# Two of eight expert weight loads split into a 112-partition transfer and five small ones

## The chip, the cores and the metric
One NeuronCore of a Trainium2 chip runs the whole kernel. The metric is device time in microseconds (us), the median of several executions; lower is better. The core has five instruction engines (PE for matmuls, DVE, ACT, POOL, SP) and 16 DMA engines that carry every transfer between HBM and the core's memory (SBUF). A transfer that POOL issues goes into the software queue q0; one that SP or ACT issues goes into a hardware queue, q1 or q10.

## What is computed
Sliding-window attention (plain in heads 0 to 3, dilated by 4 in heads 4 to 7) over 8 batches of 576 tokens, and behind it a soft mixture of experts with 32 slots, four for each of 8 experts:

```python
x = attn_out.transpose(0, 2, 1, 3).reshape(4608, 512)
logits = x @ phi                      # 4608 x 32
d = softmax(logits, axis=0); c = softmax(logits, axis=1)
slot_input = (d.T @ x).reshape(8, 4, 512)
for e in range(8):
    slot_out[e] = relu(slot_input[e] @ w1[e]) @ w2[e]   # w1: 512 x 1024, w2: 1024 x 512
return c @ slot_out.reshape(32, 512)
```

All inputs and the output are float32 in HBM. w1 and w2 of one expert are 2 MB each there, and 1 MB each as float16 in SBUF.

## The kernel before
**Stages.** The attention runs as 32 units, four for each batch (two heads at a time), each with transposes, scores, a softmax and values; the logits, token weights and slot sums of a batch follow some units behind. Then come the eight experts in pairs: `expert_in` (w1), `expert_turn` (transposes of the hidden values), `expert_out` (w2, summed into `sop`). Last, the 13 output tiles: a matmul of the token weights with `so`, a scaling by ACT or DVE into `ot`, and a store that SP issues (L791). The weights are so late, and the output so large, that the last expert's w2 and the slot output are done in two sides of 256 columns: side 0 of `so` is ready, and five output tiles' left halves are sent, before side 1 of w2 of expert 7 has arrived.

**Loads.** Apart from the first two and a table of constants, all loads are issued by POOL in an order written out by hand, because they cast float32 to float16 on the way. First the eight batches of q, k and v (`load_batch`), into eight large tiles `home0` to `home7`. When the attention has used up a home, w1 and w2 of an expert go into its two halves: in unit 4e+2, `load_w1(e)` for e up to 6 and `load_w2(e)` for e up to 4; after the loop w1 of expert 7 and w2 of experts 5, 6 and 7. For experts 0 to 5 `load_w2` is one transfer of 128 partitions; each partition is one row of 8 x 512 values, 16 KB in HBM and 8 KB in SBUF. The w2 of experts 6 and 7 are cut by columns, into three and four transfers.

**Order and limits.** POOL works in program order. The framework gives POOL's transfers eight completion semaphores in turn, so that a transfer can be issued when the one eight before it has landed. Between the weight loads POOL only clears four small tiles `hTp` (L643) for the turned hidden values. An instruction that reads a weight tile waits for the transfers that wrote it.

**Engines.** The transfers run on the 16 DMA engines at once; a transfer of 128 partitions gives each of them eight rows. Each DMA engine takes its own share from the queue in order and goes on to the next transfer without waiting for the others. A transfer has landed when all 16 have marked it complete.

Of the kernel before, what the change touches and what calls it, by code (L numbers as in the profile page):

```python
# [37 lines left out]
OUT_COLS = [sum(nj for _, nj in OUT_TILES[:i]) for i in range(len(OUT_TILES))]  # L38
NU = 4 * B
NV = 2  # L40
SIDES = ((0, DMODEL // 2), (DMODEL // 2, DMODEL))
PIECES = ((0, 6), (6, 8))
HALF = 4
# [16 lines left out]
def kernel(  # L60
# [10 lines left out]
    nc = tc.nc  # L71
# [15 lines left out]
    for n, (nm, ten, by) in enumerate((("qp", q, nc.sync), ("kp", k, nc.scalar))):  # L87
        first[nm] = stage[0:NP, 768 * n : 768 * n + 768].rearrange("p (g x) -> p g x", g=2)
        by.dma_start(
            out=first[nm],  # L90
            in_=ten[0, 0:2].rearrange("h s d -> (h s) d").rearrange("(g p r) d -> p g (r d)", g=2, r=RP),
# [3 lines left out]
    def kept(shape, name, dt=FP16):  # L95
        return keep.tile(shape, dt, name=name, tag=name)
# [24 lines left out]
    ends = kept([128, 2, 130], "ends")  # L121
    vp = [kept([128, NKB + 1, 4, D + 1], f"vp{i}") for i in range(NV)]
    vd = [kept([128, 16, D + 1], f"vd{i}") for i in range(2)]
# [9 lines left out]
    for i in range(2):  # L133
        nc.vector.memset(vd[i][:, :, D : D + 1], 1.0)
    for i in range(NV):
        nc.vector.memset(vp[i][:, :, :, D : D + 1], 1.0)
# [72 lines left out]
    def select_v(b):  # L209
        raw, last = raws[b]["vp"], raws[b]["vt"]  # L210
        for i in range(2):
            sel = ps_s.tile([128, 2, 2, 4, D], FP32, name=f"sel{b}_{i}", tag="s")
            for r in range(4):
                for n in range(2):
# [8 lines left out]
                    )  # L223
            nc.scalar.copy(out=vp[b % NV][:, 2 * i : 2 * i + 2, :, 0:D], in_=sel[:, :, 0])
        end = ring.tile([128, 2, 4, D], FP32, name=f"sel{b}_2", tag="ring")
        for r in range(4):
# [7 lines left out]
            )  # L234
        nc.scalar.copy(out=vp[b % NV][:, 4:6, :, 0:D], in_=end)

# [9 lines left out]
    def load_half(e, side):  # L246
        d0, d1 = SIDES[side]
        nc.gpsimd.dma_start(
            out=w_tiles[e][1][:, HALF:8, d0:d1],
            in_=moe_w2[e].rearrange("(p c) f -> p c f", p=128)[:, HALF:8, d0:d1],  # L250
        )

    def load_w2(e):
        w2t = w_tiles[e][1]
        w2_from = moe_w2[e].rearrange("(p c) f -> p c f", p=128)
        if e == E_EXP - 2:
            nc.gpsimd.dma_start(
                out=w2t[:, 0:HALF].rearrange("p c f -> p (c f)"),
                in_=w2_from[:, 0:HALF].rearrange("p c f -> p (c f)"),
            )  # L260
            load_half(e, 0)
            return
        if e < E_EXP - 2:
            nc.gpsimd.dma_start(
                out=w2t.rearrange("p c f -> p (c f)"), in_=w2_from.rearrange("p c f -> p (c f)")
            )
            return
        w2t = w_tiles[e][1] = w2t.rearrange("p c f -> p (c f)").rearrange("p (s c f) -> p s c f", s=2, c=8)
        for n, (d0, d1) in enumerate(SIDES):
            if n == 1:  # L270
                load_half(e - 1, 1)
            for c0, c1 in PIECES:
                nc.gpsimd.dma_start(out=w2t[:, n, c0:c1], in_=w2_from[:, c0:c1, d0:d1])
# [148 lines left out]
    def values(u):  # L422
# [11 lines left out]
        for h in range(2):  # L434
            mms = []
            for blk in range(NKB):
                if plain:
                    mms.append((blk, Pp[:, h, blk, 0:128], vp[b % NV][:, blk, hl + h, :]))
                    if blk > 0:
                        mms.append((blk, Pp[:, h, blk - 1, 128:256], vp[b % NV][:, blk - 1, hl + h, :]))  # L440
                elif blk < 4:
# [100 lines left out]
    def front_slots(b, up=None):  # L542
# [3 lines left out]
        for n in range(9):  # L546
            j = n % 4
            d0, d1 = (0, DMODEL) if n == 8 else SIDES[n // 4]
            nc.tensor.matmul(  # L549
# [15 lines left out]
    def last_slots(last, dcs):  # L565
        er, x = Er[(B - 1) % 2], xs[B - 1]
        for dc in dcs:
            to = last[:, N_SLOTS * dc : N_SLOTS * dc + N_SLOTS]
            for blk in range(4):
                for g in range(2):  # L570
                    d0, d1 = SIDES[g]
                    nc.tensor.matmul(
# [42 lines left out]
    for u in range(NU - 2):  # L615
        st = scores(u + 1)
        if u + 3 < NU:
            regroup(u + 3)
        values(u)
        softmax_parts(u + 1, st)  # L620
        if u + 3 < NU:
            transposes(u + 3)
        b, ph = divmod(u - 4, 4)
        if b >= 0:
            if ph == 1:
                front_logits(b)
            elif ph == 2:
                front_rows(b)
            elif ph == 3:
                front_slots(b)  # L630
        if u == 1:
            spread_phi()
        if u >= 1:
            x_transposes(u - 1)
        if u % 4 == 3 and u // 4 + 1 < B:
            spread_v(u // 4 + 1)
            select_v(u // 4 + 1)
        if u % 4 == 2 and u // 4 < E_EXP - 1:
            load_w1(u // 4)
            if u // 4 < E_EXP - 3:  # L640
                load_w2(u // 4)
        if 26 <= u:
            nc.gpsimd.memset(hTp[u - 26], 0.0)  # L643

    load_w1(E_EXP - 1)
    load_w2(E_EXP - 3)
    load_w2(E_EXP - 2)
    load_w2(E_EXP - 1)

# [25 lines left out]
    for c in range(2):  # L675
# [14 lines left out]
        out=siT,  # L690
# [45 lines left out]
    def expert_out(e, side=None, chs=range(8)):  # L736
        d0, d1 = (0, DMODEL) if side is None else SIDES[side]
        w2t = w_tiles[e][1][:, side] if e == E_EXP - 1 else w_tiles[e][1][:, :, d0:d1]
        for ch in chs:
            j = ch % 4  # L740
            nc.tensor.matmul(
                sop[32 * j : 32 * j + 32, d0:d1],
                hTp[e % 4][:, ch, 28 - 4 * e : 60 - 4 * e],
                w2t[:, ch, :],
                start=(e == 0 and ch < 4),
                stop=(e == E_EXP - 1 and ch >= 4),
                skip_group_check=True,
            )
# [43 lines left out]

    for n, (d0, d1) in enumerate(SIDES):
        expert_out(E_EXP - 2, n, range(HALF, 8))
# [40 lines left out]
```

## Time and profile before

| What | Value |
|---|---|
| Time, median of 3 runs | 181.5 us (181.28 to 181.54) |
| The profiled execution: its time | 181.12 us |
| The profiled execution: its span | 179.4 us |
| Busy: PE, DVE, ACT, POOL | 145.9, 124.1, 116.2, 52.9 us |
| PE clock granted, mean | 0.902 |
| q0 (POOL's transfers) | 24416 packets, 30.68 MB |
| q1 (outputs, and one first load) | 4592 packets, 9.82 MB |
| w2 as one transfer: POOL's time to issue it (L264) | 0.53 to 0.54 us |

The span is what the instruction engines' records cover; the execution's own time is 1.7 us longer. A packet record in the trace has a start, a duration, a size and a queue, but no DMA engine's number. The completion marks of each transfer are in the trace too, 16 for each transfer.

### The profile page before, as it was taken

How to read it: one execution, taken by the hardware profiler on the slowest of the kernel's cores; microseconds unless marked ns; L12 is line 12 of the kernel's file. 1: busy time of each engine (PE TensorE's matmuls, PEld its weight loads, DVE VectorE, ACT ScalarE, POOL GpSimd, SP SyncE). 2: the span in 40 equal slices, each digit the busy share in tenths (PEclk: the TensorE clock that was granted, in tenths of full speed). 3: DMA queues.
4: the chain of work that ended last, by engine and by line, in shares of the span. 5: the costliest groups of instructions: out<-in, count | busy, mean ns of one | idle time of the engine just before them, and what ended most of it. 6: DMA issues, size and time to landing. Idle time of an engine off the chain costs nothing.

```text
span 179.4 us, 5142 instructions
## 1 busy us (share of the span) xinstructions
PE 145.9 (81%) x2138; PEld 98.0 (55%) x2138; DVE 124.1 (69%) x341; ACT 116.2 (65%) x216; POOL 52.9 (30%) x86
## 2 busy tenths in 40 slices
PE   6549988999989989989998998998888997797000
PEld 2324666777576667667666757765658343342000
DVE  7407699689799978978979979876862011799200
ACT  2236768687888789789789788877721131699100
POOL 7946545454554644401110005006111100000000
PEclk9975699579999999999999999999998599999755
DMA  5999999999999999999999999999999999999995
GB/s 154 193 199 202 202 203 201 201 203 202 203 202 201 202 201 204 219 221 210 212 225 212 216 219 212 217 216 210 223 214 214 212 194 192 264 384 422 433 425 227
DMA packets 29238, 41.11 MB, mean 229 GB/s; under 512 B 1696, under 2 KB 26400, under 8 KB 26784
## 3 DMA queue, kind: packets, MB, share of 16 engines
q0 software_dynamic: 24416, 30.68, 98.0%
q1 hardware_dynamic: 4592, 9.82, 14.1%
q10 hardware_dynamic: 208, 0.29, 0.6%
q8 instruction: 16, 0.26, 0.5%
q14 instruction: 6, 0.05, 0.1%
HBM read 62.02 MB, written 9.44 MB: 398 GB/s over the span
## 4 chain that ended last, share of the span: by engine, by line
PE 30%; DMA 28%; DVE 17%; ACT 9%; issue 5%; POOL 3%; DVEq 0%; ACTq 0%; POOLq 0%
DMA home<-in_moe_w_dram 24%; PE o L448 6%; DMA home<-in_v_dram 4%; PE rgx L468 4%; ACT qT L305 4%; DVE ot L788 4%; PE sel L227 3%; PE l L486 3%; ACT pr L369 3%; PE s L343 3%; DVE x L453 3%; DVE P L395 2%; PE f L782 2%; DVE kTd L320 2%; PE u L549 2%
## 5 line engine op out<-in xcount | busy, mean ns | idle before, releaser
L453 DVE TENSOR_TENSOR x<-o,rc 128x640 f16<-128x640 f32 x32 | 26.3, 821 | 0.4
L369 ACT ACTIVATE pr<-s 128x960 f16<-128x960 f32 (+1 forms) x32 | 22.9, 761 | 1.6 <-PE s L343 1.6
L376 ACT ACTIVATE pd<-s 128x640 f16<-128x640 f32 x32 | 22.0, 713 | 2.1 <-PE s L352 2.0
L171 POOL DMA_DIRECT2D home<-in_v_dram x24 | 16.6, 692 | 14.9 <-DMA home<-in_k_dram 8.8
L448 PE MATMUL o<-vd,P 128*128 128x65 f16 x256 | 14.5, 198 | 3.2 <-DVE x L453 2.6
L240 POOL DMA_DIRECT2D home<-in_moe_w_dram x8 | 4.2, 531 | 40.8 <-PE rgq L315 33.4
L474 ACT COPY xT<-rgx 128x512 f16<-128x512 f16 x16 | 9.4, 586 | 10.2 <-PE rgx L468 10.2
L448 PEld LDWEIGHTS <-P 128*128 128x128 f16 x288 | 12.2, 100 | 6.8 <-DVE x L453 3.6
L385 DVE TENSOR_TENSOR Pp<-pr,fixed 128x1280 f16<-128x1280 f16 (+1 forms) x32 | 15.4, 497 | 0.3 <-ACT pr L369 0.3
L448 PE MATMUL o<-vp,Pp 128*128 128x65 f16 x288 | 15.3, 201 | 0.0
L468 PE MATMUL rgx<-fixed,x 128*128 128x128 f16 x155 | 14.0, 222 | 1.3 <-DVE x L453 0.6
L448 PEld LDWEIGHTS <-Pp 128*128 128x128 f16 x288 | 12.0, 102 | 4.1 <-issue 2.4
L788 DVE TENSOR_SCALAR ot<-f,rrow 128x256 f32<-128x256 f32 (+1 forms) x24 | 12.8, 610 | 2.1 <-PE f L782 2.1
L305 ACT COPY qT<-rgq 128x576 f16<-128x576 f16 x16 | 10.2, 639 | 6.1 <-PE rgq L304 5.4
L395 DVE TENSOR_TENSOR P<-pd,fixed 128x1024 f16<-128x1024 f16 x16 | 10.8, 672 | 4.7 <-ACT pd L376 4.7
L468 PEld LDWEIGHTS <-x 128*128 128x128 f16 x160 | 10.1, 98 | 6.6 <-issue 4.2
L786 ACT ACTIVATE ot<-f,rrow 128x256 f32<-128x256 f32 (+1 forms) x24 | 11.9, 601 | 2.5 <-PE f L782 1.7
L320 ACT COPY qT<-rgq 128x576 f16<-128x576 f16 x16 | 10.2, 640 | 4.1 <-PE rgq L315 4.0
L782 PE MATMUL f<-so,ET 128*128 128x256 f16 (+1 forms) x48 | 10.7, 324 | 2.3 <-ACT ot L786 1.1
L320 DVE COPY kTd<-rgk 128x576 f16<-128x576 f16 x16 | 12.3, 772 | 0.0
L197 POOL DMA_DIRECT2D home<-in_k_dram x15 | 10.0, 667 | 7.8 <-DMA home<-in_q_dram 7.1
L315 PEld LDWEIGHTS <-home 96*128 96x128 f16 x192 | 10.4, 103 | 3.3 <-DMA home<-in_q_dram 2.0
(119 smaller groups left out, 319.4 us busy)
## 6 DMA issues: line engine op xcount, KB each, us to landing
home<-in_moe_w_dram POOLq DMA_DIRECT2D x14, 1024.0 KB, 28.0
out_dram<-ot SPq DMA_DIRECT2D x5, 1024.0 KB, 7.8
home<-in_q_dram POOLq DMA_DIRECT2D x15, 288.0 KB, 9.8
home<-in_k_dram POOLq DMA_DIRECT2D x15, 288.0 KB, 9.9
home<-in_v_dram POOLq DMA_DIRECT2D x16, 256.0 KB, 9.8
out_dram<-ot SPq DMA_DIRECT2D x8, 256.0 KB, 2.9
out_dram<-ot SPq DMA_DIRECT2D x4, 512.0 KB, 7.2
home<-in_moe_w_dram POOLq DMA_DIRECT2D x2, 384.0 KB, 22.5
```

The lines of the kernel that those rows point to most:

```text
L171: nc.gpsimd.dma_start(out=dst, in_=v[b, h0 : h0 + n_h, r0 : r0 + 4 * n_p, :].rearrange("h (p r) d -> p h (r d)", r=4),)
L305: nc.scalar.copy(out=dst[:, 0:S].rearrange("c (p r) -> c p r", r=RP), in_=rg.rearrange("c r p -> c p r"),)
L320: (nc.scalar.copy if nm == "q" else nc.vector.tensor_copy)(out=dst[:, 0:S].rearrange("c (g p a) -> c g p a", g=4, a=3), in_=rg.rearrange(" ...
L369: nc.scalar.activation(out=(pr[:, :, 0 : 3 * QW], pr[:, :, 3 * QW :])[part], in_=st[:, :, 0 : (480, 224)[part]], func=AF.Exp, scale=SCALE,)
L376: nc.scalar.activation(out=pr[:, part].rearrange("p c e t -> p e c t"), in_=st[:, :, 0 : 2 * DW].rearrange("p e (c t) -> p e c t", c=2), f ...
L385: nc.vector.tensor_tensor(out=Pp[:, :, b0 : b0 + nb, 0:w], in0=pr[:, :, b0 * QW : b0 * QW + nb * w].rearrange("p h (t c) -> p h t c", c=w) ...
L395: nc.vector.tensor_tensor(out=P1.rearrange("p a c t -> p (a c) t"), in0=pr[:, :, :, 0:128].rearrange("p a c t -> p (a c) t"), in1=mask[:, ...
L448: nc.tensor.matmul(ot[:, h, blk], lhs, rhs, start=(n == 0), stop=(n == len(mms) - 1), skip_group_check=True)
L453: nc.vector.tensor_tensor(out=xs[b][:, :, 2 * D * hp : 2 * D * hp + 2 * D].rearrange("p t (h d) -> p h t d", h=2), in0=ot[:, :, :, 0:D], i ...
L468: nc.tensor.transpose(rg[:, 128 * blk : 128 * blk + 128], x[:, blk, hl : hl + 128], ident)
L782: nc.tensor.matmul(fp, ET[:, c0 : c0 + 127 * nj + 1 : nj], so[:, d0:d1], start=True, stop=True)
L788: nc.vector.tensor_scalar(out=ot[:, j], in0=fp, scalar1=scale, scalar2=None, op0=ALU.mult)
```

## The change
For experts 1 and 4 the one transfer of w2 becomes six, issued in this order. Together they name each of the 128 x 4096 values once.

```diff
+UNEVEN = (
+    (0, 112, 0, 4096), (126, 128, 0, 256), (112, 120, 0, 4096),
+    (120, 128, 256, 512), (120, 128, 512, 4096), (120, 126, 0, 256),
+)
...
         if e < E_EXP - 2:
-            nc.gpsimd.dma_start(
-                out=w2t.rearrange("p c f -> p (c f)"), in_=w2_from.rearrange("p c f -> p (c f)")
-            )
+            whole = w2t.rearrange("p c f -> p (c f)"), w2_from.rearrange("p c f -> p (c f)")
+            pieces = UNEVEN if e in (1, 4) else ((0, 128, 0, 4096),)
+            for p0, p1, x0, x1 in pieces:
+                to, of = (ap[p0:p1, x0:x1] for ap in whole)
+                nc.gpsimd.dma_start(out=to, in_=of)
             return
```

The entries of `UNEVEN` are first and last partition and first and last column. The transfer of 112 partitions is seven rows for each of 16 engines. The other five carry partitions 112 to 127. Two of them are large (eight whole rows, and eight rows of 3584 columns) and three are small (2, 8 and 6 rows of 256 columns, 512 bytes each in SBUF). If a transfer of n partitions, n below 16, takes n engines, the next ones in turn, then the leading transfer of two moves the turn on by two; the two large ones, with eight between them, fall on the same eight engines, two further than with eights alone; and after 2 + 8 + 8 + 8 + 6 = 32 the turn is where it was.

## Prediction
> **What bounds the kernel now.** I read the page's slices and queues first, then the stretch between the last load and the first output in short windows, then the timeline there, then POOL's issues.
>
> ```profile
> span 179.4 us, 5142 instructions
> ...
> DMA  5999999999999999999999999999999999999995
> ...
> q0 software_dynamic: 24416, 30.68, 98.0%
> q8 instruction: 16, 0.26, 0.5%
> q14 instruction: 6, 0.05, 0.1%
> ```
>
> The DMA engines are busy in all slices but the first and the last, so the kernel ends when the last of them has carried its share. The two lines "instruction" are program text, fetched by the same engines.
>
> ```profile
> core 0: us, PE busy (x) PEld busy (x) DVE busy (x) ACT busy (x) POOL busy (x), PEclk, DMA share, GB/s
> 151.50:152.00 0.50, 0.11 (x6) 0.10 (x1) 0.00 (x0) 0.34 (x1) 0.00 (x0) 1.00 1.44 194
> 152.00:152.50 0.50, 0.41 (x4) 0.38 (x4) 0.00 (x0) 0.14 (x2) 0.00 (x0) 1.00 1.15 155
> 153.00:153.50 0.50, 0.50 (x4) 0.31 (x4) 0.50 (x2) 0.50 (x3) 0.00 (x0) 1.00 0.83 113
> 153.50:154.00 0.50, 0.50 (x4) 0.16 (x2) 0.50 (x2) 0.50 (x3) 0.00 (x0) 1.00 0.75 99
> 154.50:155.00 0.50, 0.40 (x6) 0.11 (x6) 0.45 (x2) 0.19 (x1) 0.00 (x0) 1.00 1.10 366
> ```
>
> DMA share is the last figure but one; it passes 1 because packets overlap. From 152.0 it sinks to half of its 1.44: the engines do not finish their loads together. The last load's 16 completion marks say by how much. In us after the first they are 0, 0.05, 0.06, 0.32, 0.59, 0.86, 1.14, 1.65, 2.07, 2.28, 2.39, 2.45, 2.50, 2.59, 2.65 and 2.88.
>
> Why: q8 has 16 packets of 16 KB, 893 to 974 ns each, the last at 148.6. After each fetch the marks of the following transfers show one engine some 1.1 us later than before, and the second eight fetches hit the same eight engines as the first (their durations also repeat in eights). So eight engines are hit twice, 2.2 us each: the last eight marks. The eight others have the first eight marks. The one at 1.65 among these was already 1.22 us behind the first engine at 14 us into the span, and an 8 KB fetch of q14 (322 ns) delayed it once more.
>
> ```profile
> start us, us, engine line op out<-in xcount [idle before <-releaser]
> 150.89 0.73 PE L741 MATMUL sop<-home,hTp 128*32 128x512 f16 x16 [0.27 <-DVE hTp L731]
> 151.66 0.37 ACT L796 CAST so<-sop 128x256 f16<-128x256 f32 x1 [3.65 <-PE sop L741]
> 153.08 2.63 SPq L791 DMA_DIRECT2D out_dram<-ot  x4
> 155.24 0.29 PE L741 MATMUL sop<-home,hTp 128*32 128x256 f16 x2 [0.28 <-DMA home<-in_moe_w_dram]
> ```
>
> The first output is not held by a load: side 0 of w2 of expert 7 landed at 151.24, and PE's work of side 0, which came from the turned values (L731), ran until 151.6. SP's first store follows at 153.08 and its first packets at 154.35. Twelve engines were then idle and began at once; four still had loads and began at 154.53, 154.59, 154.67 and 154.91. From there all of them send without a pause. The first output's marks are 0.61 us apart and the last one's 0.57, with the second latest 0.26 and 0.24 before the latest. **So the latest engine alone sets the end**, with 0.56 us (154.91 less 154.35) before PE's chain would set it instead.
>
> **The change, part by part.** (1) Rows moved. A 1 MB weight transfer takes 4.87 us from landing to landing; less its closing word of 0.022 us and over eight rows this is 0.606 us for a row. The eight engines of the large pieces get 7 + 1 + 3584/4096 = 8.875 rows, the others 7 + 2 x 256/4096 = 7.125, where all had 8. For two experts that is 2 x 0.875 x 0.606 = 1.06 us more on eight engines, and 1.06 less on eight.
>
> (2) Closing words. q0 has 1248 packets of 4 bytes for 78 transfers, 16 each, 22 ns until the next packet; also for the eight v loads of 16 partitions, the narrowest. Ten more transfers cost each engine 10 x 0.022 = 0.22 us if every engine posts one, and nothing at the lower end, if only engines with data do (two words an expert in place of one come to 0.02). I take 0.22, by the nearest row.
>
> The Trainium skill (DMA: Bandwidth & Descriptors, "Why a DMA increments its semaphore by 16 and not by 1") says that on POOL's path all 16 engines post, whatever the shape. By it this term is 0.22; no trace here has a narrower transfer to show it.
>
> (3) POOL issues ten more transfers, 10 x 0.54 = 5.4 us at the price of L264, and the window of eight transfers holds fewer bytes:
>
> ```profile
> 85.70 0.53 POOL L264 DMA_DIRECT2D home<-in_moe_w_dram  x1 [4.31 <-PE rgk L315]
> 93.25 0.53 POOL L240 DMA_DIRECT2D home<-in_moe_w_dram  x1 [7.02 <-PE rgq L315]
> 107.80 0.53 POOL L240 DMA_DIRECT2D home<-in_moe_w_dram  x1 [14.02 <-PE rgq L315]
> 122.48 0.53 POOL L240 DMA_DIRECT2D home<-in_moe_w_dram  x1 [12.33 <-PE rgq L315]
> 130.44 0.77 POOL L248 DMA_DIRECT2D home<-in_moe_w_dram  x1 [3.91 <-DMA home<-in_moe_w_dram]
> ```
>
> The cover is POOL's waiting, 37.7 us in the first four rows. I walked the order with "eight before must have landed". w1 of expert 2 must then wait for w2 of expert 0 (landing 85.2), with w1 and w2 of expert 1 still queued, 10 us of work. The pieces for expert 4 go out by 111.3 (after w1 of expert 3 lands at 110.7), w1 of experts 5, 6 and 7 at 115.5, 120.6 and 125, each with two transfers of 4.87 us queued ahead. From the load at 130.44 on everything is issued as before. The clears of `hTp` behind w1 of expert 6 end by 122.9, and are needed past 143. So nothing starves, and this costs nothing. If the cover were gone, each gap would stop all 16 engines and pass to the end in full.
>
> (4) PE waits on more semaphores before `expert_out` of experts 1 and 4, at most ten more, in the stretch 144.9 to 151.6 where PE sets the output's start. Issue gaps between steps of the chain are 0.02 to 0.05 us there, so 0 to 0.5; then the first output packets are at 154.85 at worst, still before 154.91. Behind them on PE stand the last turns and side 0, which is this same delay. Cost nothing.
>
> **Sum**, if the eight engines are those without the large fetches: their latest mark becomes 1.65 + 1.06 + 0.22 = 2.93, the hit ones' latest 2.88 - 1.06 + 0.22 = 2.04. Latest before 2.88, after 2.93: +0.05 us. The profiled execution's 181.12 (its span 179.4 and 1.7 around it) would be 181.2, and the median, 0.4 above it, 181.5. With the words free it is 1.65 + 1.06 - 2.88 = -0.17. Most of the late engines gain a us, but one unhit engine takes the place of the last.
>
> **Rivals.** *Levelled: faster.* If the 1.65 engine is not late in most executions (its 1.22 us come from the start, before 14 us, where the queue is not full), the next is 1.14 + 1.06 + 0.22 = 2.42, 0.46 earlier; PE's chain stops any gain at 0.56. That gives 180.95 to 181.1. For it: the shift, 2 x 1.06 between the groups, is just the 2.2 us of two fetches. Against it: the 1.22 us stood unchanged in every transfer up to 20 us.
>
> *Wrong engines: slower.* One mechanism: a large piece falls on an engine that fetches program text. Place: the end of the loads; point: one hit engine among the eight is enough. Its price goes from 2.07 + 1.06 + 0.22 - 2.88 = +0.47 (the least late alone) to 2.88 + 1.06 + 0.22 - 2.88 = +1.28 (the latest): 182.0 to 182.8. For it: packet records have no engine number, so nothing in this trace ties the fetching engines to the turn of the pieces. Against it: a split into eight and eight exists, and the fetches repeat over eight in a fixed order, as neighbours would.
>
> *The pieces are not dealt in turn.* If each small transfer starts over at the same first engine, engines 0 to 7 get 7 + 1 + 1 = 9 rows and the rest 7, a shift of 2 x 0.606 = 1.21 us. If those eight are the unhit ones, 1.65 + 1.21 + 0.22 - 2.88 = +0.20; if not, up to +1.43: 181.7 to 182.9. For and against it the trace has nothing: no transfer has under 16 partitions.
>
> The Trainium skill (same page and section) has both rules: k consecutive engines from a round-robin cursor, and, for some direct copies from POOL, one share per engine from engine 0 on. The first is the change's own account.
>
> **Chances.** Sum as above, no change: 0.42. Levelled: 0.20. Wrong engines: 0.32, since nothing here identifies them. Not in turn: 0.06, one part in six of it unchanged. A measurement of this kernel can tell 0.2%, 0.36 us. Faster 0.20, same 0.43, slower 0.37. The likeliest case is 181.5, its own range 181.3 to 181.7. The range reaches down to the cap by PE's chain, 180.95, and up to 182.6, which leaves out the worst of the wrong engines.
>
> **What would show it.** The spread of the last load's marks: 2.9 with one mark far behind for the sum, about 2.4 if levelled, 3.4 and more with wrong engines. 1408 words of 4 bytes for step 2, POOL's issues at 85 to 130 with no drop in DMA share for step 3, and the first SP store within 0.5 us of 153.08 for step 4. A gain of over 0.6 us, or a stall of DMA between 75 and 150, would prove the account wrong.

## The result and the profile after

The changed kernel takes 182.02 us (median of 11 runs, 181.74 to 183.0) against 181.5 us before. The ratio is 1.0035, 95% interval 1.0019 to 1.0051: 0.35% slower, some 0.6 us. The profiled execution's span is 180.0 us, 0.6 longer than before.

The page of the changed kernel:

```profile
span 180.0 us, 5158 instructions
...
DMA  5999999999999999999999999999999999899995
...
DMA packets 29526, 41.11 MB, mean 228 GB/s; under 512 B 1952, under 2 KB 26688, under 8 KB 27088
...
q0 software_dynamic: 24704, 30.68, 97.7%
```

The bytes are the same, q0 has 288 packets more, and one slice near the end is no longer full. The short windows there, after the change (columns as in the prediction; DMA share is the last figure but one):

```profile
152.00:152.50 0.50, 0.16 (x2) 0.10 (x1) 0.00 (x0) 0.30 (x1) 0.00 (x0) 1.00 1.28 175
153.00:153.50 0.50, 0.50 (x4) 0.38 (x3) 0.29 (x1) 0.50 (x2) 0.00 (x0) 0.50 1.17 159
153.50:154.00 0.50, 0.50 (x4) 0.34 (x3) 0.50 (x2) 0.50 (x2) 0.00 (x0) 0.50 0.49 65
154.50:155.00 0.50, 0.50 (x4) 0.26 (x2) 0.50 (x3) 0.50 (x2) 0.00 (x0) 0.50 0.28 37
155.00:155.50 0.50, 0.50 (x10) 0.22 (x11) 0.50 (x2) 0.50 (x2) 0.00 (x0) 0.50 0.98 301
```

Before, the share sank slowly from 1.44 to 0.75. Now it holds to 153.5, then drops to 0.28, which is a fifth of the full 1.44, about three of 16 engines. The 16 marks of the last load say the same. In us after the first, and then each kernel's first, last and mean mark on its own span:

```
before  0 .05 .06 .32 .59 .86 1.14 1.65 2.07 2.28 2.39 2.45 2.50 2.59 2.65 2.88   152.32 155.19 153.85
after   0 .68 2.21 2.24 2.25 2.37 2.40 2.41 2.42 2.43 2.48 2.87 3.14 4.27 4.28 4.39   151.46 155.84 154.01
```

Two engines finish far ahead, eleven lie together, three come 1.1 us behind these. The mean moved by 0.16 us, the latest by 0.65. The marks are of one execution of each kernel, here of 181.12 and 181.74 us, both 0.3 to 0.4 us quicker than their kernel's median. In the kernels below that cost nothing, the mean mark of the profiled execution is 0.11 to 0.33 us later than before, so 0.16 is no sign of added work. Most of the loss is work in the wrong place.

The timeline of the changed kernel, where side 0 of the slot output is made:

```profile
149.33 0.51 PE L747 MATMUL sop<-home,hTp 128*32 128x512 f16 x8 [0.27 <-DVE hTp L737]
151.19 0.40 PE L747 MATMUL sop<-home,hTp 128*32 128x256 f16 x6 [1.35 <-DMA home<-in_moe_w_dram]
152.20 0.37 ACT L802 CAST so<-sop 128x256 f16<-128x256 f32 x1 [5.73 <-PE sop L747]
153.78 3.30 SPq L797 DMA_DIRECT2D out_dram<-ot  x5
```

Before, PE ran through its side 0 after the turned values. Now it waits 1.35 us for a load in the middle of it. SP's first store moved from 153.08 to 153.78, the first output packet from 154.35 to 155.05, and the last output's last mark from 178.20 to 178.81. The store is 0.70 us later and the end 0.61, so from the first store on little changes; the outputs still run without a pause.

### The profile page after: what moved, and what is told of

Its sections match the earlier page's. It is cut to its first block, busy times and chain, and to the rows that moved or that the text cites. A ratio compares the mean times of both kernels' runs of the same rounds, so it can differ in the third digit from the quotient of the medians.

```text
span 180.0 us, 5158 instructions
## 1 busy us (share of the span) xinstructions
PE 145.3 (81%) x2138; PEld 97.2 (54%) x2138; DVE 124.6 (69%) x341; ACT 116.3 (65%) x216; POOL 58.4 (32%) x96
## 4 chain that ended last, share of the span: by engine, by line
PE 36%; DVE 20%; DMA 17%; ACT 12%; issue 4%; POOL 4%; DVEq 0%; ACTq 0%; POOLq 0%
DMA home<-in_moe_w_dram 13%; PE o L454 7%; ACT pr L375 5%; ACT qT L311 5%; PE rgx L474 5%; DMA home<-in_v_dram 4%; PE l L492 4%; PE sel L231 4%; DVE x L459 4%; DVE ot L794 4%; PE f L788 3%; PE s L349 3%; DVE P L401 3%; PE u L555 2%; PE sel L220 2%
## 5 line engine op out<-in xcount | busy, mean ns | idle before, releaser
L272 POOL DMA_DIRECT2D home<-in_moe_w_dram x16 | 8.3, 524 | 22.9 <-DMA home<-in_moe_w_dram 14.0
L788 PE MATMUL f<-so,ET 128*128 128x256 f16 (+1 forms) x48 | 11.4, 360 | 2.3 <-ACT ot L792 1.1
L244 POOL DMA_DIRECT2D home<-in_moe_w_dram x8 | 4.4, 554 | 22.5 <-DVE Pp L391 7.6
```

What stands on the lines that cost most here:

```text
L788: nc.tensor.matmul(fp, ET[:, c0 : c0 + 127 * nj + 1 : nj], so[:, d0:d1], start=True, stop=True)
```

## The experiments

Three theories were on trial. "In turn": the small transfers are dealt to the next engines, so the large pieces sit on the eight two further (the change's own account, and the base of the sum). "Same engines": each small transfer starts over at the same first engine. "Cost of splitting": more transfers cost time whatever they carry. Each ratio below is to runs of the kernel before on the same chip, whose medians were 181.45 to 181.62 us.

The first evidence is in the changed kernel's own packets. On a busy engine the next packet starts a fixed time after the last one (606 ns after a whole row, 530 after one of 7168 bytes, 41 after one of 512, 21 to 22 after a word), so an engine's packets can be followed from start to start. One engine of the changed kernel, in us of its span:

```
92.380 row of 8192 bytes | 92.985 word | 93.006 512 bytes | 93.046 word | 93.067 7168 bytes | 93.597 word | 93.618 512 bytes | 93.658 word
```

That is a row of the first large piece, one of the small eight, one of the second large piece, one of the six. All 16 packets of 7168 bytes have a whole row and a 512-byte packet ahead on their engine, and twelve of the 16, six of eight at each expert, have a 512-byte packet behind. At expert 1, where the chains can be told apart, two of the eight have one ahead of the whole row as well: the share of the leading transfer of two. Dealt in turn, the 512-byte packets of the small eight would be on the other eight engines. At expert 4 eight engines show only words there, eleven each: the closing word of the 112 rows and two for each of the five small transfers.

**Two whole eights** (experts 1 and 4, as in the change):

```diff
-    (0, 112, 0, 4096), (126, 128, 0, 256), (112, 120, 0, 4096),
-    (120, 128, 256, 512), (120, 128, 512, 4096), (120, 126, 0, 256),
+    (0, 112, 0, 4096), (112, 120, 0, 4096), (120, 128, 0, 4096),
```

> Experts 1 and 4: 112 rows, then two transfers of 8 whole rows, nothing cut by columns. Theory 'in turn' (the next eight engines follow the last): the two eights fall on different halves, all 16 engines carry 8 rows, and only four more closing words are paid (4 x 0.022 = 0.09 us): 181.6 us, the last load's 16 marks spread over 2.9 us as before. Theory 'same engines' (each transfer of 8 starts over at the same first engine): eight engines carry 9 rows and eight carry 7, 2 x 0.606 = 1.21 us more and less, as in the changed kernel: 182.0 us, the marks spread over 4.2 to 4.5 us. Theory 'cost of splitting' (more transfers, whatever they carry): two of five extra transfers an expert, so two fifths of the loss, 181.7 us, marks 2.9 us.

Measured: 182.18 us, ratio 1.0051 (1.0032 to 1.0069); the marks spread over 4.76 us, the mean at 154.04. The windows of this kernel:

```profile
153.50:154.00 0.50, 0.48 (x4) 0.21 (x2) 0.50 (x2) 0.50 (x3) 0.00 (x0) 1.00 0.57 76
154.00:154.50 0.50, 0.50 (x4) 0.34 (x3) 0.50 (x3) 0.50 (x2) 0.00 (x0) 1.00 0.43 57
154.50:155.00 0.50, 0.50 (x6) 0.11 (x6) 0.50 (x3) 0.50 (x3) 0.00 (x0) 1.00 0.27 36
```

The same drop to 0.27 with nothing cut by columns and four extra transfers in place of ten. Two eights make 16, but they do not cover 16 engines. "In turn" has fallen, and with it my sum.

**Plain eights**, the change without its leading transfer of two:

```diff
-    (0, 112, 0, 4096), (126, 128, 0, 256), (112, 120, 0, 4096),
-    (120, 128, 256, 512), (120, 128, 512, 4096), (120, 126, 0, 256),
+    (0, 112, 0, 4096), (112, 120, 0, 4096), (120, 128, 256, 512),
+    (120, 128, 512, 4096), (120, 128, 0, 256),
```

> The changed kernel without the transfer of 2 rows ahead; the transfer of 6 becomes one of 8. So 112, 8 large, 8 small, 8 large, 8 small, with the same rows in all. 'In turn': the large ones sit two engines back from the changed kernel's; the set of late engines changes by up to four of 16, so the spread of the marks must differ from the changed kernel's 4.4 us, and the time from 182.0 by some tenths of a us. 'Same engines': leading the turn by two does nothing; the same eight engines carry 9 rows, 182.0 us, marks 4.4 us, each P (7168-byte packet) preceded on its engine by a whole row and followed by a 512-byte one in all 16 cases. 'Cost of splitting': 181.9 us, and marks 2.9 us.

Measured: 182.2 us, ratio 1.0043 (1.0026 to 1.0061); marks over 4.67 us, again with two engines far ahead (0 and 0.19, the next at 2.24). The interval overlaps the change's own. Followed from start to start, 15 of the 16 packets of 7168 bytes stand in the sequence row, 512 bytes, 7168 bytes, 512 bytes (the other one is next to a fetch), and eight engines at each expert show only words. Leading by two makes no difference that these runs can tell.

**Sixteens**, six transfers that load all engines alike:

```diff
-    (0, 112, 0, 4096), (126, 128, 0, 256), (112, 120, 0, 4096),
-    (120, 128, 256, 512), (120, 128, 512, 4096), (120, 126, 0, 256),
+    (0, 48, 0, 4096), (48, 64, 0, 4096), (64, 80, 0, 4096),
+    (80, 96, 0, 4096), (96, 112, 0, 4096), (112, 128, 0, 4096),
```

> Experts 1 and 4: six transfers again, but 48 rows and five times 16, so that all 16 engines carry 8 rows by either way of dealing. 'Cost of splitting': the whole loss stays, 182.0 us. 'In turn' and 'same engines': only the ten closing words, 10 x 0.022 = 0.22 us on the latest engine: 181.7 us, marks spread over 2.9 us.

Measured: 182.49 us, ratio 1.0056 (1.0037 to 1.0076), as slow as the change. This spoke for "cost of splitting". But the place differs:

```profile
153.50:154.00 0.50, 0.50 (x4) 0.33 (x3) 0.00 (x0) 0.21 (x1) 0.00 (x0) 0.50 0.86 116
154.50:155.00 0.50, 0.50 (x4) 0.35 (x3) 0.50 (x2) 0.50 (x2) 0.00 (x0) 0.50 0.74 99
155.00:155.50 0.50, 0.50 (x5) 0.34 (x3) 0.50 (x2) 0.50 (x3) 0.00 (x0) 0.50 0.45 59
```

The share sinks slowly, as before the change, only about a us later: the mean mark is at 154.69, +0.84 us, where the change has +0.16. All engines are late. The packet records say why: 77 of the 1792 whole rows took over 650 ns, up to some 950, 61 of them starting at 90 to 92 and 120 to 123 us, where the sixteens run; before it was ten, next to fetches. The time over 626 ns comes to 0.68 us an engine, against 0.13. The extra 0.55 and ten words of 0.022 us are 0.77 of the 0.84. Five transfers of 16 neighbouring partitions, one behind the other, stretched their packets; why is not shown. The changed kernel has no such stretch (0.14 us over 626 ns). So this run was no clean control.

**Fours**, expert 1 alone:

```diff
+    (0, 112, 0, 4096), (112, 116, 0, 4096), (116, 120, 0, 4096),
+    (120, 124, 0, 4096), (124, 128, 0, 4096),
...
+            pieces = UNEVEN if e in (1,) else ((0, 128, 0, 4096),)
```

> Expert 1 alone: 112 rows, then four transfers of 4 whole rows. 'In turn': all engines carry 8 rows, four more words, 181.6 us, marks 2.9 us. 'Same engines': four engines carry 11 rows, +3 x 0.606 = 1.82 us, and twelve carry 7, -0.61 us. Four marks move up by 2.42 us against the other twelve. If two of the four fetch program text, two marks stand about 2.1 + 1.82 = 3.9 to 4.0 us on the scale of before, where the latest is 2.88: about +1.1 us, 182.6 us; if none does, the latest is at most 1.65 + 1.82 + 0.09 = 3.6: +0.7 us; if all do, up to +1.9 us.

Measured once: 182.46 us, the latest mark at 156.32, 1.12 us later than before. The order of size is that of "same engines", and the packets show it: four engines carry four single whole rows each, with one word between. The marks (…, 3.18, 3.64, 4.34) do not tell how many of the four fetch: the first mark of an execution and the lags from its start differ by some tenths of a us, and one execution can't settle it.

**One sixteen**, the clean control: the first experiment with its two eights as one transfer:

```diff
-    (0, 112, 0, 4096), (112, 120, 0, 4096), (120, 128, 0, 4096),
+    (0, 112, 0, 4096), (112, 128, 0, 4096),
```

> As the first experiment, but the two transfers of 8 rows are one of 16: all engines carry 8 rows again. 'Same engines' (uneven rows are the loss): two more words, 2 x 0.022 = 0.04 us, and at most 0.06 us for 16 rows that go to neighbouring partitions (the five such transfers of an expert in the third experiment stretched packets by 0.55 us an engine in ten): 181.5 to 181.6 us, within 0.1% of before, marks spread near 2.9 us. 'Cost of splitting' (a second transfer on these partitions is the loss): most of the first experiment's +0.5%, 182.0 us or more.

Measured: 181.62 us, ratio 0.9998 (0.9986 to 1.0010); marks over 3.23 us, the mean at 153.95. Its windows sink slowly, as before the change:

```profile
153.50:154.00 0.50, 0.50 (x4) 0.38 (x3) 0.50 (x3) 0.50 (x2) 0.00 (x0) 0.56 0.87 117
154.00:154.50 0.50, 0.50 (x7) 0.09 (x6) 0.50 (x2) 0.50 (x3) 0.00 (x0) 0.50 0.52 69
```

Its whole rows spent no more over 626 ns than before (0.12 us an engine), so one transfer of 16 partitions by itself is not slow. The same partitions and the same bytes: as 8 + 8 they cost 0.51%, as 16 nothing. Splitting as such is not the loss; giving eight engines nine rows and eight engines seven is.

**Smaller shifts.** If unequal rows are the loss, a smaller shift might be a gain, since most of the late engines are among those that get fewer rows. Three kernels change expert 1 alone:

```diff
+# eights, expert 1
+    (0, 112, 0, 4096), (112, 120, 0, 4096), (120, 128, 0, 4096),
...
+# part shift
+    (0, 112, 0, 4096), (112, 128, 0, 1024), (112, 120, 1024, 4096), (120, 128, 1024, 4096),
...
+# ten and six
+    (0, 112, 0, 4096), (112, 128, 0, 1024), (112, 122, 1024, 4096), (122, 128, 1024, 4096),
```

> The first experiment's split for expert 1 alone: eight engines carry one row more, eight one less, 0.61 us each way. 'Same engines', with two of the first eight fetching program text and six of the others (as the packet chains of the experiments so far say): the two move from about 2.0 to 2.6, the one late unhit engine from 1.65 to 2.3, the six from 2.88 to 2.27 at the latest, so the latest mark falls from 2.88 to about 2.65 with the words: -0.2 us, 181.2 to 181.3 us. 'Cost of splitting': half the first experiment's loss, 181.9 us.

> Expert 1 alone, 112 rows, then 1024 columns of the last 16 rows in one transfer, and the other 3072 columns in two transfers of 8 rows: 0.75 of a row more on eight engines and less on eight, 0.45 us each way. 'Same engines': the two hit ones of the first eight at 2.0 + 0.45, the six at 2.88 - 0.45 = 2.43, and 0.07 us of words: about -0.35 us, 181.1 to 181.2 us. 'In turn': no row moves, +0.07 us, 181.5 us. 'Cost of splitting': +0.5 us, 182.0 us.

> As the last one, with the 3072 columns in transfers of 10 and 6 rows. 'Same engines': the first six engines 0.45 us more, the next four as before, the last six 0.45 us less. If the six hit engines outside the first eight are just the last six, the latest mark falls as in the last experiment, -0.35 us, 181.1 to 181.2 us, and the two engines that lead by 0.6 us and more there are not seen to lead here. If the last six hold unhit engines, hit ones stay where they were, and the time is that of before, 181.5 us. 'Cost of splitting': +0.5 us.

Measured: 181.61 us, ratio 0.9999 (0.9989 to 1.0009); 181.48 us, 0.9995 (0.9985 to 1.0006); 181.35 us, 0.9987 (0.9975 to 0.9998). The first of them has half the shift of the two eights and half their extra transfers, and none of their loss; a price for each transfer would leave half of it. The hoped gains of 0.2 to 0.35 us came to nothing, nothing that can be told, and 0.13%. The last is the only one of these ten kernels that is faster than before, by 0.24 us; its interval ends close to 1, so this can be chance. The hit engines among the first eight were later than I took them for (2.0 us): in the first of the three runs the last marks are 3.34, 3.42 and 3.66, counted from an engine that has lost a row, which is 2.73 to 3.05 on the scale of before.

**Fourteen and two**, to learn which engines of the first eight fetch:

```diff
-    (0, 112, 0, 4096), (126, 128, 0, 256), (112, 120, 0, 4096),
-    (120, 128, 256, 512), (120, 128, 512, 4096), (120, 126, 0, 256),
+    (0, 112, 0, 4096), (112, 126, 0, 4096), (126, 128, 0, 4096),
```

> Experts 1 and 4: 112 rows, then transfers of 14 and of 2 whole rows. 'Same engines': the first two engines carry 9 rows (+1.21 us in all), the next twelve 8, the last two 7. If the two hit engines of the first eight are the very first two, they move from 2.1 to 2.3 up to 3.3 to 3.5, with 0.09 us of words 0.5 to 0.7 us behind the latest of before: 182.1 us, a ratio near 1.003. If they stand elsewhere among the eight, the first two are unhit and reach at most 1.65 + 1.21 + 0.09 = 2.95: 181.5 to 181.7 us, a ratio near 1.000. 'In turn': all carry 8 rows, 181.6 us.

Measured: 181.63 us, ratio 1.0003 (0.9988 to 1.0018). So the very first two engines are not the two hit ones ("hit": they fetch program text). The run is also the closest control for the number of transfers: like the two eights it cuts the last 16 rows of both experts into two transfers of whole rows, and 14 + 2 costs nothing. Its marks spread over 4.35 us all the same, the first at 151.45 and the last at 155.80. That is as late as in the change's profile, but there it was the quickest execution of eleven (181.74 us), here a middling one (181.75, of 181.35 to 181.96). I had hoped to find them there, since then the eight engines two further would have been the right ones; this run speaks against that.

## Why the prediction was wrong

**The bound** was read rightly: the kernel ends when the latest DMA engine has carried its share. The latest mark moved by 0.65 us, and the end by 0.61 (178.20 to 178.81).

**Step 1 failed**, and with it the sum: "The eight engines of the large pieces get 7 + 1 + 3584/4096 = 8.875 rows, the others 7 + 2 x 256/4096 = 7.125". The small pieces are not dealt in turn. All five transfers begin at one and the same engine, so eight engines carry nine rows (within a sixteenth) and eight carry seven. The shift is 2 x 0.606 = 1.21 us, not 1.06. This was the third rival, "the pieces are not dealt in turn", with a chance of 0.06 and 181.7 to 182.9 us; the measured 182.02 lies in it. It lies in the range of the whole, 180.95 to 182.6, too, but only by the width that the rivals gave it: the forecast was no change. The page of the Trainium skill that I cited (DMA: Bandwidth & Descriptors, "Why a DMA increments its semaphore by 16 and not by 1") has both rules; by the second, some direct copies from POOL put the number of partitions over 16, rounded up, on each engine from engine 0 on, and under 16 rows that is one row to an engine. These runs agree with the second for transfers of 2, 6 and 8 rows, as far as they show it: one first engine for all, whatever its number. Four transfers of 4 rows fell on four engines. I gave the other rule the weight because the change counted on it, which is no evidence.

**Which engines.** The sum's condition, "if the eight engines are those without the large fetches", failed as well, and it costs more: with the dealing alone put right and the eight unhit, the third rival has +0.20 us. In the changed kernel only two engines finish far ahead, at 0 and 0.68 us: unhit engines with seven rows. Since eight are unhit, six of them are among those with nine rows, and two of those with nine are hit. These two, and the unhit engine that was late from the start, are the three at 4.27 to 4.39. The packets bear this out. Counted from the first of them, the eight packets of 7168 bytes start at 0, 0.11, 0.13, 0.15, 0.49, 0.95, 1.00 and 1.45 us at expert 1, and at 0, 0.16, 0.20, 0.23, 0.90, 1.50, 2.06 and 2.14 us at expert 4. Read most simply, the two at 0.95 and 1.00 have fallen back by 1.1 us, a fetch each, and the others by less than half of that. The two with the share of the leading two rows are at 0.13 and 0.49, so they are not the hit ones, as in the last experiment. Put right, the step gives 2.07 + 1.21 + 0.22 - 2.88 = +0.62 us for a hit engine with the earliest of the hit marks; measured +0.65. That engine is picked after the fact, and the latest would give +1.43, so the agreement is partly luck. The spread of 4.39 us is the sign that the prediction named for wrong engines (3.4 and more). So "wrong engines" was half of the truth too: the point from which it decides, one hit engine among the eight, was passed.

**Step 2, the closing words**, was right for the engines that decide and wrong in the count: 1504 words, not 1408. With a row in each piece an engine spends 21 to 22 ns on each word, so ten take the 0.22 us. An engine without a row in a transfer carries two words for it (48 such shares an expert), but short ones: where it had no row in all five small transfers, their ten words took some 0.06 us together.

**Step 3 held.** POOL's waits covered the ten issues, and the queue never ran dry:

```profile
91.86 0.54 POOL L272 DMA_DIRECT2D home<-in_moe_w_dram  x1 [5.38 <-PE rgq L321]
...
116.03 0.58 POOL L244 DMA_DIRECT2D home<-in_moe_w_dram  x1 [4.96 <-DVE Er L529]
...
131.05 0.78 POOL L252 DMA_DIRECT2D home<-in_moe_w_dram  x1 [1.83 <-DMA home<-in_moe_w_dram]
```

These are POOL's issues of w2 of expert 2, w1 of expert 5 and the load that was issued at 130.44 before. POOL waits ahead of each, so the issues have room. w1 of expert 5 goes out at 116.0 where I had 115.5, and the last of the six pieces for expert 4 was out at 111.1, where I had 111.3. The DMA share from 75 to 100, 100 to 125 and 125 to 150 us is 1.04, 1.03 and 1.09 (before 1.03, 1.03 and 1.10).

**Step 4**, PE's added waits, can't be seen: the wait that took their place is the load of side 0, 1.35 us. I had read side 0 as PE's own, with 0.4 us to spare; a load that is 0.65 us later uses that up, and the first store follows it, 0.70 us later where the prediction allowed 0.5.

**The levelled rival** put a cap of 0.56 us on any gain. The best kernel here has 0.24, so no run tests the cap.

What stays open: which two of the first eight engines fetch program text, beyond that they are not the first two; why transfers of 16 partitions in a row stretch packets; and whether any form of these transfers would be dealt in turn.

## What to carry to other kernels

Before a transfer is cut to move work between DMA engines, find out how small transfers are dealt, with two transfers of eight rows against one of sixteen: here that pair, 1.0051 against 0.9998, decided more than the whole arithmetic. Here all transfers of 2 to 8 rows loaded the same first engines, so a split that looked even by partitions was uneven by engines. And look at a transfer's completion marks one by one, the latest above all: their spread shows that work was moved, not that time was lost. 14 + 2 spread them as widely as the change, 4.35 us, and cost nothing. The marks are of one execution, so the times of several decide.

## What was not expected of the hardware

- Transfers of 16 neighbouring partitions, five behind each other, stretched whole-row packets from 625 ns to as much as 950, 0.55 us an engine over ten of them, though each engine had one row of each. A single one of them did not.
- An engine that has no row of a transfer still carries two words for it, most of them of 9 ns in place of 22: some 0.011 us a transfer.
- After PE's wait of 1.35 us the granted clock fell to 0.50 from 153.0 on (before 1.00 there), and the twelve matmuls of side 0 took 2.68 us in place of 2.01. No run shows whether the wait caused this. It did not decide: the two eights kept 1.00 there and were as slow, and the one sixteen fell to 0.50 and lost nothing.
